# Funnel attention with a routed feed-forward: small PSUM results read by ScalarE, two transposes and the loads issued earlier, the stores of x later

## The chip, the cores and the metric

The kernel runs on one core of a Trainium2 chip. The metric is the device time of one launch in microseconds (us): the median of three runs before the change is 805.76 us (804.05 to 808.37).

## The reference

Inputs are q, k and v of shape (8, 8, 1152, 64) in fp32 (batch, heads, positions, head width), a gate vector of 512, weights w1 (512 x 1024) and w2 (1024 x 512), and a capacity of 128.

```
q_pool = q.reshape(B, H, 576, 2, 64).mean(axis=3)        # pairs of queries are averaged
attn   = softmax(q_pool @ k^T / sqrt(64)) ; out = attn @ v
x      = out with the heads side by side                 # (8, 576, 512)
per batch b:
  scores = x[b] @ w_gate
  top    = the 128 tokens with the largest scores
  x[b, top] += sigmoid(scores[top]) * (relu(x[b, top] @ w1) @ w2)
```

## The kernel before

The class `_Plain` does all the work. Its unit is a **pair** of heads of one batch: the two heads' 64 columns fill 128 partitions, so there are 8 x 4 = 32 pairs. The 576 pooled queries of a pair are cut into two **halves** of 288: the even half (s = 0) and the odd half (s = 1), 64 in all. `run` (L1098 on) goes over the halves with index h, and in iteration h it writes down, in this order:

- in an odd half, the loads of k, q and v of the pair after next (`load_pair`, ten DMAs issued by SP);
- `scores(h)`: nine chunks of 128 keys. A chunk is one matmul per head (L747, four PE instructions in the trace) into one PSUM tile of two banks; ScalarE turns it into exponentials p (L754, 128 x 576);
- `gated(h - 2)`: gate products of an earlier half summed (L861); after the odd half of a batch's last pair it also starts that batch's routing, with the DMA that copies x to the output and the tile diag (L894);
- `folded(h)`: the sums of p over the keys. POOL adds two thirds (acc, L779, three instructions), DVE folds the rest and then acc (L784, twice) and sums (L793);
- `weighted(h - 1)`: p times v (L762, 36 PE instructions), copied out of PSUM by ScalarE (av, L770); `drained(h - 1)`: a transpose (avb, L807) and the product with the gate vector on POOL (prod, L810);
- in an even half, `prepare_pair`: the sum of query pairs on POOL (qp, L726) and the transposes kT and qT on DVE (L729, L733) for the pair that comes next;
- in an even half, `normalized` of the pair just finished: one matmul that merges the sums (L822), 1e-9 added while DVE reads it out of PSUM (L832, two instructions), the reciprocal rec (L840), x on POOL (L842), and four DMAs on SP that store x to the DRAM tile xs (L850);
- `units`: one step of the routing of each batch under way.

Routing (`routed`, L876 on) is a generator that is stopped at each `yield True` until the next half. Its steps: the gate scores spread over all partitions by a matmul with ones (L905, it reads diag); the scores turned into columns by five tiny transposes (L664) that DVE reads out of PSUM (L668, L669); ranks by comparison on DVE; the pick matrix; the index matmul (L983), read out of PSUM by DVE (L991, L993), and an indirect DMA that gathers the 128 picked rows (xe, L995); their transposes (L1008); the first layer (L1019, 64 instructions) and the second (L1032, 16), DVE's sum (L1041) and an indirect DMA that scatters the rows into the output (L1049). The steps of a batch fall into the next batch's first halves, so each stands at a fixed place of every batch but the first.

Each engine runs its instructions in the order in which the program writes them; a wait on one holds what is behind it. All PSUM tiles come from one pool of four (`banks`), so a score chunk shares it with av, the merge, the columns, the index and the feed-forward. Which of the four a tile gets is settled when the program is built.

Of the kernel before, what the change touches and what calls it, by code (L numbers as in the profile page):

```python
# [10 lines left out]
P = 128  # L11
# [3 lines left out]
F32 = mybir.dt.float32  # L15
I32 = mybir.dt.int32
AF = mybir.ActivationFunctionType
ALU = mybir.AluOpType
# [516 lines left out]
class _Plain:  # L535
# [62 lines left out]
    def constants(self):  # L598
        nc, const = self.nc, self.const
# [24 lines left out]
        )  # L624
        line_f = self.ffn.tile([1, self.Sp], F32, name="sc_row")
        nc.vector.tensor_copy(line_f[:, :], line_i.rearrange("p n i -> p (n i)"))
        self.token = const.tile([P, self.NT], F32, name="token")
        self.columns(self.token, line_f, self.banks()[:, 0, :])

# [10 lines left out]
            self.merge[:, :, :], self.same[:, :].unsqueeze(1).broadcast_to([P, P // BLK, BLK])  # L640
        )

        self.meta = const.tile([P, self.B, self.NT, 3], F32, name="meta")
# [14 lines left out]

    def columns(self, to, line, ps):

        nc, NF = self.nc, self.NF
        for t in range(self.NT):
            rows = P if t < NF else self.TAIL
            nc.tensor.transpose(  # L664
                ps[0:rows, t : t + 1], line[0:1, t * P : t * P + rows], self.ident[0:1, 0:1]
            )
        nc.vector.memset(to[:, NF : NF + 1], 0.0)
        nc.vector.tensor_copy(to[:, 0:NF], ps[:, 0:NF])  # L668
        nc.vector.tensor_copy(to[0 : self.TAIL, NF : NF + 1], ps[0 : self.TAIL, NF : NF + 1])  # L669

# [146 lines left out]
    def normalized(self, pair):  # L817


        nc, hb, hp = self.nc, self.HB, pair["hp"]  # L820
# [9 lines left out]
        for j in range(2):  # L830
            rows = slice(j * self.D, (j + 1) * self.D)
            nc.vector.tensor_scalar(  # L832
                out=tot[rows, :].rearrange("p (s n) -> p s n", s=2),
                in0=ps[rows, 0 : 4 * hb].rearrange("p (s j n) -> p s j n", s=2, j=2)[:, :, j, :],
                scalar1=1e-9,
                scalar2=None,
                op0=ALU.add,
            )
# [7 lines left out]
            op=ALU.mult,  # L846
        )
        for j, ds, rows in self.quarters():
            d0 = (2 * hp + j) * self.D
            nc.sync.dma_start(  # L850
                pair["xs"][:, d0 + ds.start : d0 + ds.stop].rearrange("(i n) d -> i n d", i=BLK),
                x[rows, :, :],
            )
# [25 lines left out]
    def routed(self, b, xs, part):  # L879
# [20 lines left out]
        yield  # L900
        sc_row = ffn.tile([P, 2, self.HALF], F32, name="sc_row")
        flat = diag.rearrange("p n i -> p (n i)")
        ps = self.banks()
        for s in range(2):
# [6 lines left out]
            )  # L911
        nc.scalar.copy(sc_row[:, :, :], ps[:, :, 0 : self.HALF])
        sc_row = sc_row.rearrange("p s n -> p (s n)")
        yield True
        sc = ffn.tile([P, NT], F32, name="gate_sc")
        self.columns(sc, sc_row, self.banks()[:, 0, :])
        gate = ffn.tile([P, NT], F32, name="gate")

        nc.vector.tensor_scalar(
            out=gate[:, :], in0=sc[:, :], scalar1=-88.0, scalar2=None, op0=ALU.max  # L920
# [48 lines left out]
        for s0, w in self.slots:  # L969
# [12 lines left out]
            for t, rows in tiles:  # L982
# [7 lines left out]
            index = ffn.tile([P, 2], I32, name="index")  # L990
            nc.vector.tensor_copy(index[0:w, :], ps[0:w, 0:2])  # L991
            own_gate = ffn.tile([P, 1], F32, name="own_gate")
            nc.vector.tensor_copy(own_gate[0:w, :], ps[0:w, 2:3])  # L993
            xe = ffn.tile([P, self.Dm], F32, name="xe")
# [6 lines left out]
                oob_is_err=False,  # L1001
            )
            yield True

# [97 lines left out]
    def run(self):  # L1102
# [10 lines left out]
        for h in range(n_halves + 1):  # L1113
            if h < n_halves:
                n, s = divmod(h, 2)
                if s == 0:
                    pair = upcoming
                    if pair["hp"] == 0:
                        xs = self.dram.tile([self.Sp, self.Dm], F32, name="xs")
                        part = self.ffn.tile([P, self.NPAIR, self.QB], F32, name="part")  # L1120
                    pair.update(xs=xs, part=part)
                elif n + 2 < len(pairs):
                    loaded = self.load_pair(*pairs[n + 2])
                else:
                    loaded = None
                if h > 1:
                    next(weights, None)
                half = {"pair": pair, "s": s}
                halves.append(half)
                self.scores(half)  # L1130
                if h > 1:
                    self.gated(halves[h - 2])
                self.folded(half)
            elif h > 1:
                self.gated(halves[h - 2])
            if h > 0:
                done = halves[h - 1]
                self.weighted(done)
                self.drained(done)
            if h < n_halves and s == 0 and loaded:  # L1140
                upcoming = loaded
                self.prepare_pair(upcoming)
            if h > 0 and done["s"] == 1:
# [3 lines left out]
        for _ in weights:  # L1147
            pass


# [87 lines left out]
```

## Time and profile before

| | before |
|---|---|
| median of 3 runs | 805.76 us |
| the profiled execution, device time | 803.0 us |
| its span, first to last instruction | 801.3 us |
| TensorE (PE) busy | 760.9 us, 95% |
| VectorE (DVE) busy | 541.9 us, 68% |
| GpSimd (POOL) busy | 422.1 us, 53% |
| ScalarE (ACT) busy | 372.7 us, 47% |
| mean granted TensorE clock | 0.993 of full speed |

The profiled execution is one launch; 1.7 us of its time lie outside the span. Busy time of PE is not work at its peak, since matmuls are pipelined and a block that waits between its instructions still shows as nearly busy. So the blocks of PE are compared with each other: the same 36 instructions in one place and in another.

### The profile page before, as it was taken

The page shows a single profiled execution, that of the slowest core. Times are in us where ns is not written, and L with a number is a line of the kernel's source. Part 1 is how long each engine was busy: PE and PEld are TensorE (multiplying, and loading weights), DVE is VectorE, ACT ScalarE, POOL GpSimd, SP SyncE. Part 2 cuts the span into 40 slices and gives each one's busy share as a digit, 9 for nine tenths or more (in the row PEclk, how much of TensorE's full clock was granted, in tenths as well). Part 3 has the DMA queues.
Part 4 walks back from the last instruction along what each step waited for, and adds up shares of the span by engine and source line. Part 5 has one row for each costly group of instructions (what it writes and reads, how often), then busy time and mean ns, then how long its engine had stood idle before and what let it go on. Part 6 is the DMA issues. An engine that isn't in the chain of part 4 may idle for free.

```text
span 801.3 us, 14111 instructions
## 1 busy us (share of the span) xinstructions
PE 760.9 (95%) x5503; PEld 475.7 (59%) x5503; DVE 541.9 (68%) x888; ACT 372.7 (47%) x681; POOL 422.1 (53%) x372
## 2 busy tenths in 40 slices
PE   6999989999999999999999899998999999999896
PEld 4666546566565655657556575565755657556564
DVE  4666679964698637896288762987539876398560
ACT  5555555533555335553455444554435553355310
POOL 5666666563555636655265643665536645266320
PEclk9999999999999999999999999999999999999899
DMA  9677785567155671556725557355565555450120
GB/s 156 140 154 160 156 189 105 105 117 159 28 98 101 117 163 39 95 93 114 163 53 104 95 102 162 62 92 106 100 143 86 96 92 104 125 104 16 29 88 31
DMA packets 453643, 84.97 MB, mean 106 GB/s; under 512 B 450752, under 2 KB 450752, under 8 KB 453312
## 3 DMA queue, kind: packets, MB, share of 16 engines
q1 hardware_dynamic: 446976, 79.13, 51.8%
q0 software_dynamic: 1280, 4.20, 1.7%
q10 hardware_dynamic: 5312, 0.66, 0.5%
q8 instruction: 45, 0.74, 0.4%
q14 instruction: 30, 0.25, 0.1%
HBM read 72.42 MB, written 20.97 MB: 117 GB/s over the span
## 4 chain that ended last, share of the span: by engine, by line
PE 39%; POOL 20%; issue 18%; DVE 9%; DMA 7%; ACT 4%; SPq 3%; POOLq 0%; ACTq 0%
PE ps L747 15%; POOL acc L779 13%; PE ps L762 12%; PE ps L1019 5%; PE ps L1032 4%; POOL qp L726 4%; ACT p L754 4%; DMA xe<-xs,index 3%; DVE fold L784 2%; DMA out_dram<-xs 2%; POOL x L842 1%; POOL prod L810 1%; DVE qT L733 1%; DMA v_sb<-in_v_dram 1%; DVE part L863 1%
## 5 line engine op out<-in xcount | busy, mean ns | idle before, releaser
L754 ACT ACTIVATE p<-ps 128x576 f32<-128x576 f32 x576 | 325.8, 679 | 97.0 <-PE ps L747 48.0
L747 PE MATMUL ps<-qT,kT 64*128 64x288 f32 x2304 | 326.4, 426 | 17.9 <-ACT p L754 12.3
L762 PE MATMUL ps<-p,v_sb 128*64 128x288 f32 x2304 | 293.5, 409 | 0.0
L779 POOL TENSOR_TENSOR acc<-p 128x576 f32<-128x576 f32 x192 | 266.5, 1416 | 28.5 <-ACT p L754 28.2
L747 PEld LDWEIGHTS ps<-qT,kT 64*128 64x128 f32 x2304 | 205.1, 188 | 125.8 <-ACT p L754 71.3
L762 PEld LDWEIGHTS ps<-p,v_sb 128*64 128x64 f32 x2304 | 159.8, 137 | 125.6 <-ACT p L754 24.2
L784 DVE TRANSPOSE_TENSOR_REDUCE fold<-p 128x54 f32<-128x1728 f32 x64 | 126.1, 1970 | 78.2 <-ACT p L754 78.2
L810 POOL TENSOR_TENSOR prod<-avb,w_gate 128x288 f32<-128x288 f32 x64 | 51.0, 796 | 209.8 <-DVE avb L807 194.9
L784 DVE TRANSPOSE_TENSOR_REDUCE fold<-acc 128x54 f32<-128x1728 f32 x64 | 125.2, 1957 | 50.5 <-POOL acc L779 50.4
L770 ACT COPY av<-ps 128x288 f32<-128x288 f32 x64 | 25.5, 398 | 229.2 <-PE ps L762 229.2
L842 POOL TENSOR_TENSOR x<-avb,rec 128x576 f32<-128x576 f32 x32 | 37.0, 1157 | 44.6 <-DVE rec L840 34.4
L1019 PE MATMUL ps<-xeT,w 128*128 128x128 f32 x512 | 59.6, 276 | 0.6 <-ACT xeT L1011 0.6
L1019 PEld LDWEIGHTS ps<-xeT,w 128*128 128x128 f32 x512 | 58.0, 192 | 0.8 <-ACT xeT L1011 0.7
L1032 PE MATMUL ps<-w,hT 128*128 128x512 f32 x128 | 56.5, 593 | 0.0
L726 POOL TENSOR_TENSOR qp<-qb 128x576 f32<-128x576 f32 (+1 forms) x33 | 45.1, 1366 | 7.2 <-DMA qb<-in_q_dram 7.1
L733 DVE STREAM_TRANSPOSE qT<-qp 128x576 f32<-128x576 f32 (+1 forms) x33 | 25.1, 760 | 34.4 <-POOL qp L726 34.4
L1041 DVE SCALAR_TENSOR_TENSOR xe<-ps,own_gate,xe 128x512 f32<-128x512 f32 x8 | 6.0, 751 | 59.0 <-PE ps L1032 59.0
L1049 POOL DMA_INDIRECT out_dram<-xe,index x8 | 8.3, 1034 | 70.2 <-DMA out_dram<-xs 35.1
L729 DVE STREAM_TRANSPOSE kT<-kb 128x1152 f32<-128x1152 f32 (+1 forms) x33 | 43.0, 1302 | 3.1 <-DMA kb<-in_k_dram 3.1
L1032 PEld LDWEIGHTS ps<-w,hT 128*128 128x128 f32 x128 | 24.1, 190 | 27.0 <-issue 26.3
L861 DVE TENSOR_REDUCE red<-prod 128x9 f32<-128x288 f32 x64 | 28.0, 437 | 11.2 <-POOL prod L810 11.2
L1027 ACT ACTIVATE hT<-ps 128x512 f32<-128x512 f32 x16 | 9.6, 597 | 53.3 <-PE ps L1019 53.3
(66 smaller groups left out, 332.1 us busy)
## 6 DMA issues: line engine op xcount, KB each, us to landing
v_sb<-in_v_dram SPq DMA_DIRECT2D x64, 288.0 KB, 4.1
kb<-in_k_dram SPq DMA_DIRECT2D x124, 144.0 KB, 3.2
qb<-in_q_dram SPq DMA_DIRECT2D x124, 144.0 KB, 3.5
xs<-x SPq DMA_DIRECT2D x128, 72.0 KB, 2.2
out_dram<-xs SPq DMA_DIRECT2D x8, 1152.0 KB, 7.5
w<-in_moe_w_dram SPq DMA_DIRECT2D x8, 512.0 KB, 5.5
kb<-in_k_dram SPq DMA_DIRECT2D x8, 72.0 KB, 3.0
qb<-in_q_dram ACTq DMA_DIRECT2D x8, 72.0 KB, 3.1
```

What stands on the lines that cost most here:

```text
L726: nc.gpsimd.tensor_tensor(out=qp[:, qs, :], in0=pair["q"][:, qs, 0, :], in1=pair["q"][:, qs, 1, :], op=ALU.add)
L729: nc.vector.transpose(pair["kT"][:, i * nk * BLK : (i + 1) * nk * BLK], pair["k"][:, ks, :].rearrange("p n d -> p (n d)"),)
L733: nc.vector.transpose(pair["qT"][:, i * nq * BLK : (i + 1) * nq * BLK], qp[:, qs, :].rearrange("p n d -> p (n d)"),)
L747: nc.tensor.matmul(sc[:, j, 0:n], lhsT=pair["kT"][rows, c * P : (c + 1) * P], rhs=pair["qT"][rows, qs], start=True, stop=True,)
L754: nc.scalar.activation(p[:, c // G, c % G, :, :], sc[:, :, 0:n], AF.Exp, scale=self.scale)
L762: nc.tensor.matmul(av[j * self.D : (j + 1) * self.D, 0:n], lhsT=half["pair"]["v"][:, j, c, :], rhs=half["p"][:, c // G, c % G, j, :], star ...
L779: nc.gpsimd.tensor_tensor(out=acc[:, u, :], in0=units[:, 0, u, :], in1=units[:, 1, u, :], op=ALU.add)
L784: nc.vector.tensor_reduce(fold[:, a, :], of.rearrange("p u (m d) -> p (u m) d", d=BLK), AX.X, ALU.add, apply_transpose=True,)
L810: nc.gpsimd.tensor_tensor(out=pair["prod"][:, ns, :], in0=pair["avb"][:, ns, :], in1=self.w_gate[:, hp : hp + 1, :].broadcast_to([P, hb, B ...
L842: nc.gpsimd.tensor_tensor(out=x[:, :, :], in0=pair["avb"][:, :, :], in1=rec[:, :].unsqueeze(2).broadcast_to([P, self.QB, BLK]), op=ALU.mult,)
L1019: nc.tensor.matmul(pv[:, f, 0:w], lhsT=self.w1[:, c, (f0 + f) * P : (f0 + f + 1) * P], rhs=xeT[:, c, 0:w], start=(c == 0), stop=(c == self ...
L1032: nc.tensor.matmul(ps[0:w, 0 : self.Dm], lhsT=hT[:, f, 0:w], rhs=self.w2[:, f, :], start=(f == 0), stop=(f == self.NFC - 1),)
```

## The change

Four things are done. First, small results that DVE read out of PSUM are read by ScalarE: the merged sums (an Identity activation with a bias tile `tiny` that holds 1e-9), the columns (now five full transposes from a row of 640 whose tail POOL fills with zeros, and one copy), the index and the gate of the picked rows. The lower bound of the gate moves from DVE to POOL. Second, `prepare_pair` is called right behind the even half's `folded`, ahead of `weighted` and `drained`. Third, the stores of x become a function `stored`, called an odd half later and behind the loads; before, `normalized` issued them ahead of the loads. Fourth, routing gets one more `yield True` behind the gather, so the transposes of the picked rows and both layers come a half later, and one more call of `units` stands ahead of the last `weighted`.

```
-    def columns(self, to, line, ps):
+    def line_of_scores(self):
+        line = self.ffn.tile([P, self.NT * P], F32, name="sc_row")
+        self.nc.gpsimd.memset(line[0:1, self.Sp :], 0.0)
+        return line
+    def columns(self, to, line):
+        ps = self.banks()[:, 0, 0 : self.NT]
         for t in range(self.NT):
...
-                ps[0:rows, t : t + 1], line[0:1, t * P : t * P + rows], self.ident[0:1, 0:1]
-            )
-        nc.vector.memset(to[:, NF : NF + 1], 0.0)
-        nc.vector.tensor_copy(to[:, 0:NF], ps[:, 0:NF])
-        nc.vector.tensor_copy(to[0 : self.TAIL, NF : NF + 1], ps[0 : self.TAIL, NF : NF + 1])
+                ps[:, t : t + 1], line[0:1, t * P : (t + 1) * P], self.ident[0:1, 0:1]
+            )
+        nc.scalar.copy(to[:, :], ps)
...
     def normalized(self, pair):
-            nc.vector.tensor_scalar(
-                out=tot[rows, :].rearrange("p (s n) -> p s n", s=2),
-                in0=ps[rows, 0 : 4 * hb].rearrange("p (s j n) -> p s j n", s=2, j=2)[:, :, j, :],
-                scalar1=1e-9,
-                scalar2=None,
-                op0=ALU.add,
+            nc.scalar.activation(
+                tot[rows, :].rearrange("p (s n) -> p s n", s=2),
+                ps[rows, 0 : 4 * hb].rearrange("p (s j n) -> p s j n", s=2, j=2)[:, :, j, :],
+                AF.Identity,
+                bias=self.tiny[rows, 0:1],
             )
...
+        pair["x"] = x
+    def stored(self, pair):
         for j, ds, rows in self.quarters():
-            nc.sync.dma_start(
+            self.nc.sync.dma_start(
                 pair["xs"][:, d0 + ds.start : d0 + ds.stop].rearrange("(i n) d -> i n d", i=BLK),
-                x[rows, :, :],
+                pair["x"][rows, :, :],
             )
...
-        nc.vector.tensor_scalar(
+        nc.gpsimd.tensor_scalar(
             out=gate[:, :], in0=sc[:, :], scalar1=-88.0, scalar2=None, op0=ALU.max
         )
...
-            nc.vector.tensor_copy(index[0:w, :], ps[0:w, 0:2])
+            nc.scalar.copy(index[0:w, :], ps[0:w, 0:2])
-            nc.vector.tensor_copy(own_gate[0:w, :], ps[0:w, 2:3])
+            nc.scalar.copy(own_gate[0:w, :], ps[0:w, 2:3])
...
+            yield True
             yield True
             xeT = ffn.tile([P, self.ND, P], F32, name="xeT")
...
-                elif n + 2 < len(pairs):
-                    loaded = self.load_pair(*pairs[n + 2])
                 else:
-                    loaded = None
+                    loaded = self.load_pair(*pairs[n + 2]) if n + 2 < len(pairs) else None
+                    if n > 0:
+                        self.stored(halves[h - 2]["pair"])
...
                 self.folded(half)
+                if s == 0 and loaded:
+                    upcoming = loaded
+                    self.prepare_pair(upcoming)
             elif h > 1:
                 self.gated(halves[h - 2])
+            if h == n_halves:
+                self.units()
             if h > 0:
                 done = halves[h - 1]
                 self.weighted(done)
                 self.drained(done)
-            if h < n_halves and s == 0 and loaded:
-                upcoming = loaded
-                self.prepare_pair(upcoming)
```

On ScalarE, around the even half that turns a batch's scores into columns, before the change:

```order
L912 COPY sc_row<-ps 128x576
L754 ACTIVATE p<-ps 128x576 x9
L770 COPY av<-ps 128x288
L754 ACTIVATE p<-ps 128x576 x9
L770 COPY av<-ps 128x288
```

and of the changed program, at the same place:

```order
L920 COPY sc_row<-ps 128x576
L760 ACTIVATE p<-ps 128x576 x9
L776 COPY av<-ps 128x288
L837 ACTIVATE sums<-ps,tiny 64x18 x2
L675 COPY gate_sc<-ps 128x5
L760 ACTIVATE p<-ps 128x576 x9
L776 COPY av<-ps 128x288
```

The two reads of the merged sums and the one of the columns now stand between a copy of av and the next nine exponentials.

On VectorE, one pair of the first batch, from an even half's second fold on, before:

```order
L784 TENSOR_REDUCE fold<-acc 128x54
L793 TENSOR_REDUCE sum<-fold 128x18
L807 STREAM_TRANSPOSE avb<-av 128x288
L729 STREAM_TRANSPOSE kT<-kb 128x1152
L733 STREAM_TRANSPOSE qT<-qp 128x576
L832 TENSOR_SCALAR sums<-ps 64x18 x2
L840 RECIPROCAL rec<-sums 128x18
L861 TENSOR_REDUCE red<-prod 128x9
L863 TENSOR_TENSOR part<-red,rec 128x18
```

and of the changed program:

```order
L790 TENSOR_REDUCE fold<-acc 128x54
L799 TENSOR_REDUCE sum<-fold 128x18
L735 STREAM_TRANSPOSE kT<-kb 128x1152
L739 STREAM_TRANSPOSE qT<-qp 128x576
L813 STREAM_TRANSPOSE avb<-av 128x288
L844 RECIPROCAL rec<-sums 128x18
L869 TENSOR_REDUCE red<-prod 128x9
L871 TENSOR_TENSOR part<-red,rec 128x18
```

The transposes kT and qT moved ahead of avb, and the two reads of sums are gone from this queue.

On TensorE, the second half of a batch's routing and the start of the next one (the picked rows xe, the first layer xeT, the spread scores diag, the second layer hT, the columns sc_row), before:

```order
L1008 MATMUL ps<-ident,xe 128x128 x4
L747 MATMUL ps<-qT,kT 128x288 x18
L762 MATMUL ps<-p,v_sb 64x288 x18
L822 MATMUL ps<-sum,merge 128x36
L1019 MATMUL ps<-xeT,w_126 128x128 x32
L747 MATMUL ps<-qT,kT 128x288 x18
L762 MATMUL ps<-p,v_sb 64x288 x18
L905 MATMUL ps<-diag,ones 128x288 x2
L1032 MATMUL ps<-w_127,hT 128x512 x8
```

and of the changed program:

```order
L827 MATMUL ps<-sum,merge 128x36
L1018 MATMUL ps<-ident,xe 128x128 x4
L753 MATMUL ps<-qT,kT 128x288 x18
L768 MATMUL ps<-p,v_sb 64x288 x18
L913 MATMUL ps<-diag,ones 128x288 x2
L1029 MATMUL ps<-xeT,w_127 128x128 x32
L753 MATMUL ps<-qT,kT 128x288 x18
L768 MATMUL ps<-p,v_sb 64x288 x18
L827 MATMUL ps<-sum,merge 128x36
L672 MATMUL ps<-ident,sc_row 128x1 x5
L1042 MATMUL ps<-w_128,hT 128x512 x8
```

The first layer moved from ahead of the matmul on diag to behind it, and the second layer now stands between the columns and an odd half's scores.

## Rows read from the trace of the kernel before

**Rows 1.** The page: busy time (share of the span), instructions.

```profile
PE 760.9 (95%) x5503; PEld 475.7 (59%) x5503; DVE 541.9 (68%) x888; ACT 372.7 (47%) x681; POOL 422.1 (53%) x372
```

**Rows 2.** Timeline, PE, most of a batch: start, us, line, op, idle before.

```profile
299.73 4.64 PE L747 MATMUL ps<-qT,kT 64*128 64x288 f32 x36
...
309.51 1.24 PE L747 MATMUL ps<-qT,kT 64*128 64x288 f32 x8
311.07 1.30 PE L747 MATMUL ps<-qT,kT 64*128 64x288 f32 x8 [0.31 <-ACT p L754]
...
316.27 4.59 PE L762 MATMUL ps<-p,v_sb 128*64 128x288 f32 x36
320.79 4.72 PE L747 MATMUL ps<-qT,kT 64*128 64x288 f32 x36
...
348.85 0.41 PE L822 MATMUL ps<-sum,merge 128*128 128x36 f32 x2
349.10 1.23 PE L983 MATMUL ps<-meta,pick 128*128 128x3 f32 x9
...
357.04 4.59 PE L762 MATMUL ps<-p,v_sb 128*64 128x288 f32 x36
...
372.49 7.39 PE L1019 MATMUL ps<-xeT,w 128*128 128x128 f32 x64
379.81 5.03 PE L747 MATMUL ps<-qT,kT 64*128 64x288 f32 x36
```

**Rows 3.** Timeline, PE, the last pair's odd half.

```profile
739.66 1.23 PE L983 MATMUL ps<-meta,pick 128*128 128x3 f32 x9
...
744.68 6.04 PE L747 MATMUL ps<-qT,kT 64*128 64x288 f32 x28 [2.60 <-DVE sums L832]
750.66 1.68 PE L762 MATMUL ps<-p,v_sb 128*64 128x288 f32 x12
```

**Rows 4.** Waits: engine, line, waited for: us in total, times, longest us.

```profile
PE ps L1008 <- DMA xe<-xs,index: 7.3, 7, 1.7
PE ps L905 <- DVE diag L894: 3.6, 1, 3.6
```

**Rows 5.** Waits of SP's queue.

```profile
SPq L850 <- POOL x L842: 358.4, 32, 20.9
```

**Rows 6.** Timeline, ACT, an odd half behind the columns and a plain one.

```profile
212.72 1.19 ACT L754 ACTIVATE p<-ps 128x576 f32<-128x576 f32 x2 [1.04 <-PE ps L747]
...
233.50 5.00 ACT L754 ACTIVATE p<-ps 128x576 f32<-128x576 f32 x9 [0.68 <-PE ps L747]
```

**Rows 7.** Lines by form: busy us, mean ns of one | idle before.

```profile
L770 ACT COPY av<-ps 128x288 f32<-128x288 f32 x64 | 25.5, 398 | 229.2 <-PE ps L762 229.2
...
L832 DVE TENSOR_SCALAR sums<-ps 64x18 f32<-64x18 f32 x64 | 10.3, 162 | 0.8
...
L961 ACT ACTIVATE gate<-gate 128x5 f32<-128x5 f32 x8 | 1.7, 210 | 0.0
...
L754 ACT ACT_TABLE_LOAD x1 | 1.3, 1283 | 8.9 <-DMA qb<-in_q_dram 8.9
```

**Rows 8.** Timeline, DVE, first batch: two folds one pair apart, and diag.

```profile
65.47 1.98 DVE L784 TRANSPOSE_TENSOR_REDUCE fold<-acc 128x54 f32<-128x1728 f32 x1 [2.22 <-POOL acc L779]
...
85.07 1.98 DVE L784 TRANSPOSE_TENSOR_REDUCE fold<-acc 128x54 f32<-128x1728 f32 x1 [2.22 <-POOL acc L779]
...
97.83 0.78 DVE L733 STREAM_TRANSPOSE qT<-qp 128x576 f32<-128x576 f32 x1 [1.01 <-POOL qp L726]
...
100.89 1.59 DVE L894 TENSOR_TENSOR diag<-line,same 128x576 f32<-128x576 f32 x1
```

**Rows 9.** Timeline, POOL, beside that diag.

```profile
100.48 4.65 POOL L779 TENSOR_TENSOR acc<-p 128x576 f32<-128x576 f32 x3
```

**Rows 10.** Timeline, a later batch: diag on DVE, and PE's matmul on it.

```profile
282.05 0.76 DVE L894 TENSOR_TENSOR diag<-line,same 128x576 f32<-128x576 f32 x1
...
291.69 1.24 PE L905 MATMUL ps<-diag,ones 128*128 128x288 f32 x4
```

More of the change, by code (lines that the diff above doesn't have):

```diff
@@ L624, in constants @@
         )
-        line_f = self.ffn.tile([1, self.Sp], F32, name="sc_row")
-        nc.vector.tensor_copy(line_f[:, :], line_i.rearrange("p n i -> p (n i)"))
+        line_f = self.line_of_scores()
+        nc.vector.tensor_copy(line_f[0:1, 0 : self.Sp], line_i.rearrange("p n i -> p (n i)"))
         self.token = const.tile([P, self.NT], F32, name="token")
-        self.columns(self.token, line_f, self.banks()[:, 0, :])
+        self.columns(self.token, line_f)
         self.same = const.tile([P, BLK], F32, name="same")
@@ L641, in constants @@
         )
+        self.tiny = const.tile([P, 1], F32, name="tiny")
+        nc.gpsimd.memset(self.tiny[:, :], 1e-9)
         self.meta = const.tile([P, self.B, self.NT, 3], F32, name="meta")
@@ L657, in constants @@
         self.w2 = const.tile([P, self.NFC, self.Dm], F32, name="w2")
-    def columns(self, to, line, ps):
-        nc, NF = self.nc, self.NF
+    def line_of_scores(self):
[3 more added lines that the diff above has]
+    def columns(self, to, line):
+        nc = self.nc
+        ps = self.banks()[:, 0, 0 : self.NT]
         for t in range(self.NT):
-            rows = P if t < NF else self.TAIL
             nc.tensor.transpose(
-                ps[0:rows, t : t + 1], line[0:1, t * P : t * P + rows], self.ident[0:1, 0:1]
+                ps[:, t : t + 1], line[0:1, t * P : (t + 1) * P], self.ident[0:1, 0:1]
             )
-        nc.vector.memset(to[:, NF : NF + 1], 0.0)
-        nc.vector.tensor_copy(to[:, 0:NF], ps[:, 0:NF])
-        nc.vector.tensor_copy(to[0 : self.TAIL, NF : NF + 1], ps[0 : self.TAIL, NF : NF + 1])
+        nc.scalar.copy(to[:, :], ps)
     def load_gate(self):
@@ L847, in normalized @@
         )
+        pair["x"] = x
+    def stored(self, pair):
         for j, ds, rows in self.quarters():
-            d0 = (2 * hp + j) * self.D
-            nc.sync.dma_start(
+            d0 = (2 * pair["hp"] + j) * self.D
+            self.nc.sync.dma_start(
                 pair["xs"][:, d0 + ds.start : d0 + ds.stop].rearrange("(i n) d -> i n d", i=BLK),
-                x[rows, :, :],
+                pair["x"][rows, :, :],
             )
@@ L900, in routed @@
         yield
-        sc_row = ffn.tile([P, 2, self.HALF], F32, name="sc_row")
+        sc_row = self.line_of_scores()
         flat = diag.rearrange("p n i -> p (n i)")
@@ L911, in routed @@
             )
-        nc.scalar.copy(sc_row[:, :, :], ps[:, :, 0 : self.HALF])
-        sc_row = sc_row.rearrange("p s n -> p (s n)")
+        nc.scalar.copy(
+            sc_row[:, 0:Sp].rearrange("p (s n) -> p s n", s=2), ps[:, :, 0 : self.HALF]
+        )
         yield True
         sc = ffn.tile([P, NT], F32, name="gate_sc")
-        self.columns(sc, sc_row, self.banks()[:, 0, :])
+        self.columns(sc, sc_row)
         gate = ffn.tile([P, NT], F32, name="gate")
-        nc.vector.tensor_scalar(
+        nc.gpsimd.tensor_scalar(
             out=gate[:, :], in0=sc[:, :], scalar1=-88.0, scalar2=None, op0=ALU.max
@@ L1148, in run @@
             pass
+        self.stored(halves[-1]["pair"])
         self.gated(halves[-1])
```

## The prediction

> **What bounds the kernel now.** The page comes first: PE is busy 95% of the span, no other engine above 68% [rows 1]. So a microsecond is won only where PE's own instructions move closer together, and the second view is PE's timeline over one batch, where equal blocks are compared. An even half's scores take 4.64 us for 36 instructions [rows 2]; printed durations overlap the next instruction by 0.07 to 0.08 (4.64 here, the next block begins 4.56 later), so 4.56 is what such a block costs. The same block takes 5.03 in most odd halves. The odd half behind the columns runs from 309.51 to 316.27, 6.76: its instructions come in eights, 1.51 apart, each eight (two chunks) waiting for ScalarE's exponentials. The index matmul and the odd half behind it take from 349.10 to 357.04, 7.94. The reader is to see that PE waits only for ScalarE in these rows, yet ScalarE is not full: it needs 5.00 for nine exponentials [rows 6] and there it takes longer. I read it as the number of the four PSUM tiles that the chunks can use. Two tiles for nine chunks give pairs in lockstep; three give ScalarE's own pace of 5.0; four let PE run ahead at 4.56. The tiles that are missing are the ones that DVE reads: the merge in every odd half, with it the columns or the index in two of four. In the last odd half PE waits for that read by name, 2.60 us for sums L832 [rows 3].
>
> Then the table of waits: PE waits 7.3 us in seven places for the gathered rows, 3.6 once for diag [rows 4]. Last, the queues that nobody on PE waits for: SP stood 358.4 us, one wait a pair, in front of the stores of x, with the loads behind them [rows 5].
>
> **The change part by part**, on the profiled execution, 803.0 us (span 801.3 and 1.7 around it).
>
> *The reads go to ScalarE.* Behind the copy of av they are ready at once, the tiles come free before the first exponentials, and all four serve the chunks. Of the 31 odd halves behind a merge:
> - 17 are blocks of 5.03 like the one at 379.81: 5.03 - 4.64 = 0.39 each, 6.6 us.
> - 7 stand behind the columns, 6.76 each. The first batch's falls to 4.56, 2.20. In the other six the second layer now stands in between, and its tile is still read by DVE; I keep the three-tile pace of 4.95 for them, 1.81 each, 10.9. Together 13.1; if that tile is free too, 2.3 more.
> - 6 stand behind the index: of 7.94, 6.76 are scores as behind the columns, so 1.18 the index; 1.18 + 4.56 = 5.74, 2.20 each, 13.2. The seventh, the last odd half, takes 11.00 (739.66 to 750.66 [rows 3]) and saves 5.26. Together 18.5.
> - 7 even halves behind the columns take 4.72 instead of 4.64: 0.6.
>
> What ScalarE pays: two reads of 64 x 18 a pair and one or two small copies in the odd halves named. The nearest rows are 0.21 (128 x 5, not from PSUM) and 0.40 (128 x 288 from PSUM) [rows 7]; I take 0.21, since the sizes are near it. They stand where ScalarE is idle, 0.68 in a plain odd half and 1.04 behind the columns [rows 6]: 0.42 of 0.68, 0.63 of 1.04, so nothing. At 0.40 each, 0.80 would stick out by 0.12 in 32 places, 3.8 us. The waits that these reads add hold the exponentials behind them, but they are for matmuls that stand ahead of those scores on PE. [...]
>
> *One more half between gather and transposes.* The seven waits of 7.3 us go: a half lasts some 9 us, the longest wait was 1.7.
>
> *The transposes ahead of avb.* This works through DVE's chain, second fold, sum, avb, kT, qT, sums, rec, red, part, line, diag. In the first batch it comes round every 19.60 us (65.47 to 85.07 [rows 8]), while PE's pair takes 2 x 4.51 (316.27 to 320.79) + 4.56 + 4.95 + 0.25 for the merge (348.85 to 349.10 [rows 2]) = 18.8: DVE falls behind 0.8 a pair until PE waits 3.60 for diag. The change takes from the chain the wait of qT for qp (1.01) and the two reads (2 x 0.162 = 0.32) and adds an estimated 0.6, since red now waits for a prod that starts later; 0.7 to 0.8 less, 18.8 to 18.9. But PE's pair falls to 18.4. So DVE still falls behind by 0.45 a pair; over the four pairs the wait shrinks by 4 x 0.35 to 2.2: 1.4 saved.
>
> *What is late next: diag in every later batch.* Today none of them waits, because the first layer, 7.32 us of PE (372.49 to 379.81), stands ahead of the matmul on diag; it moves behind it. There diag is done at 282.81 and PE arrives at 291.69, 8.88 later [rows 10]; without the first layer 1.56 are left. PE also arrives earlier by what is saved in the two halves or three before, 2.20 + 0.39 + 7.3 / 7 = 3.6, DVE by two rounds of 0.75. And diag, 0.76 now, then runs beside POOL's acc, as in the first batch, where it took 1.59 [rows 8] while three acc, elsewhere 4.14, took 4.65 [rows 9]: 0.83 more. -1.56 + 3.6 - 1.5 + 0.83 = 1.4; I take 1.5 in each of six batches, 9.0 lost. Its ends are 0 and the 3.60 of the first batch. (The seventh is the program's end, where the order on PE stays.)
>
> [...]
>
> *Loads at once, stores behind them.* PE never waits for k, q or v in this stretch, so earlier loads win nothing. The stores leave some ten issues later; their reader, the gather, comes four halves on, and that is the cover. If it went, PE would wait for the rows as in [rows 4], about 1 us in seven batches. POOL's extra gate bound and fills, 8 x 0.3 and less, lie in its idle time.
>
> **Sum.** 6.6 + 13.1 + 18.5 + 0.6 + 7.3 + 1.4 - 9.0 = 38.5. 803.0 - 38.5 = 764.5. The median of the runs lies 2.8 above the profiled execution, so 767.3; I say 767.
>
> **The rivals.**
> - *DVE becomes the bound.* The round of 18.85 does not keep up with 18.4, the ranks stand in the same queue, and each of six batches waits the full 3.60: 21.6 instead of 9.0, and nothing of the first 3.60 saved. Of the gains 46.1 are left. 803.0 - 46.1 + 21.6 = 778.5, in runs 781. For it: the first batch shows it. Against it: the first layer alone gives DVE 7.3 us a batch to catch up, and DVE is rid of 10.3 us of sums and of the columns' reads.
> - *The tiles are not the reason.* Odd halves stay at 5.03 and 6.76, because ScalarE's pace sets them; then 7.3 and 1.4 are won and up to 9.0 lost: no change, 803.0, in runs 806. For it: every row of those blocks names ScalarE. Against it: even halves run at 4.56 with the same nine exponentials.
> - *ScalarE swaps its function table.* The new Identity stands between two runs of exponentials. If each change of function loaded a table at the 1.28 of [rows 7], it would be 64 loads on ScalarE, ahead of the scores' exponentials: 82 us, 764.5 + 82 = 846.5, in runs 849, slower. It decides from 38.5 / 64 = 0.60 us a change. Against it: the program before copies with ScalarE between exponentials 64 times and shows one load. [...]
>
> **How the numbers follow.** The forecast holds 0.80, DVE as the bound 0.13, tiles not the reason 0.04, tables 0.03. The forecast's own range: all waits on diag at 0, with six faster odd halves, gives 767.3 - 9.0 - 2.2 - 2.3 = 754; diag late by twice as much (9.0) and ScalarE at 0.40 (3.8) give 780. With DVE as the bound the upper end is 781. Range 754 to 781. About 0.5% is what a measurement can tell from no change; the first two cases are faster, the third is the same, the fourth slower, and I leave 0.01 more to same: faster 0.92, same 0.05, slower 0.03.
>
> **What would show it.** Right: odd halves' scores of 36 instructions at 4.64 instead of 5.03, those behind the index likewise; no wait of PE for xe; no reads of sums on DVE; ACT with one table load; PE waiting for diag in most batches, 1 to 2 us. Wrong: eights 1.51 apart that stay, more than one table load, or diag waits above 3 us. The prediction falls if ScalarE's small reads take far more than 0.4, or if the earlier loads and the ordering of POOL's work push acc, and with it the folds, behind PE so that the merge matmul itself waits.

## The result, and the profile after

The changed kernel takes **773.0 us** (median of 4 runs, 772.3 to 773.7), the kernel before 806.0 in the same round (804.1 to 808.4): ratio 0.959, 95% interval 0.956 to 0.962. The forecast was 767 with a range of 754 to 781. The profiled execution took 773.65 us with a span of 771.9, against 803.0 and 801.3; these two differ by 29.4, the medians by 33.0, since before's profiled execution lay 3.0 below its median and the changed kernel's 0.6 above.

The page answers [rows 1] so (busy us, share of the span, instructions):

```profile
PE 740.6 (96%) x5503; PEld 492.6 (64%) x5503; DVE 526.1 (68%) x773; ACT 388.0 (50%) x770; POOL 425.9 (55%) x390
```

PE is busy 20.3 us less with the same number of matmuls, ScalarE 15.3 more, DVE 15.8 less. PE's timeline over most of a batch answers [rows 2 and 10] (start, us, line, op, idle before):

```profile
237.19 4.63 PE L753 MATMUL ps<-qT,kT 64*128 64x288 f32 x36
...
246.27 0.41 PE L827 MATMUL ps<-sum,merge 128*128 128x36 f32 x2
246.51 1.23 PE L992 MATMUL ps<-meta,pick 128*128 128x3 f32 x9
...
252.26 4.59 PE L768 MATMUL ps<-p,v_sb 128*64 128x288 f32 x36
...
277.68 1.21 PE L913 MATMUL ps<-diag,ones 128*128 128x288 f32 x4 [1.86 <-DVE diag L902]
278.72 7.31 PE L1029 MATMUL ps<-xeT,w 128*128 128x128 f32 x64
...
295.38 0.47 PE L672 MATMUL ps<-ident,sc_row 1*128 1x1 f32 x5
295.78 7.13 PE L1042 MATMUL ps<-w,hT 128*128 128x512 f32 x16
302.84 5.03 PE L753 MATMUL ps<-qT,kT 64*128 64x288 f32 x36
```

From the index matmul to the next weighted products is 5.75 us where it was 7.94. The odd half that follows both the columns and the second layer is at 5.03, still ScalarE's pace (5.00 for nine exponentials). The new stop is in front of diag's matmul. The waits, which answer [rows 3 and 4]:

```profile
PE ps L913 <- DVE diag L902: 11.4, 6, 2.3
PE ps L753 <- DVE qT L739: 7.4, 2, 4.2
...
PE ps L1018 <- DMA xe<-xs,index: 1.0, 2, 0.7
```

No row of PE names the sums any more. On ScalarE the reads appear, with one table load, against [rows 7]; and SP's queue, against [rows 5], now stands in front of the loads, since the keys' buffer is not yet transposed:

```profile
L837 ACT ACTIVATE sums<-ps,tiny 64x18 f32<-64x18 f32 x64 | 17.4, 272 | 1.0
...
L675 ACT ACT_TABLE_LOAD x1 | 1.3, 1283 | 5.3 <-DMA qb<-in_q_dram 5.3
```

```profile
SPq L705 <- DVE kT L735: 223.0, 31, 12.9
SPq L858 <- POOL x L846: 33.3, 2, 16.9
```

What the prediction had no term for stands at the program's start, PE again. Before, the second scores began at 23.39 and the first merge at 32.47, without a gap. In the changed kernel:

```profile
8.76 11.18 PE L753 MATMUL ps<-qT,kT 64*128 64x288 f32 x72 [4.21 <-DVE qT L739]
19.87 4.59 PE L768 MATMUL ps<-p,v_sb 128*64 128x288 f32 x36
27.62 7.53 PE L753 MATMUL ps<-qT,kT 64*128 64x288 f32 x36 [3.17 <-DVE qT L739]
35.08 4.59 PE L768 MATMUL ps<-p,v_sb 128*64 128x288 f32 x36
39.60 0.41 PE L827 MATMUL ps<-sum,merge 128*128 128x36 f32 x2
```

The first merge is 7.1 us late. And SP's DMA queue (packets, MB, share of 16 engines' time), with the landing time of a pair's quarter of the keys, moved the same bytes in much more engine time; before, the share was 51.8% and the landing 3.2 us:

```profile
q1 hardware_dynamic: 446976, 79.13, 69.7%
...
kb<-in_k_dram SPq DMA_DIRECT2D x124, 144.0 KB, 4.6
```

Block by block on PE (start of a block to start of the next, from the two timelines):

| what | places | before | forecast | after |
|---|---|---|---|---|
| plain odd halves | 17 | 4.95 | 4.56 | 4.57 |
| odd half, first batch's columns | 1 | 6.77 | 4.56 | 4.57 |
| odd half, later columns | 6 | 6.76 | 4.95 | 4.95 (one 5.23) |
| index + odd half | 6 | 7.94 | 5.74 | 5.75 |
| the same, last | 1 | 11.00 | 5.74 | 5.74 |
| waits for gathered rows, in all | 7 | 7.3 | 0 | 1.0 |
| wait for diag, first batch | 1 | 3.6 | 2.2 | 0 |
| waits for diag, later, in all | 6 | 0 | 9.0 | 11.4 |
| first merge begins at | 1 | 32.47 | no term | 39.60 |

The differences, 6.5 + 2.2 + 10.6 + 13.1 + 5.3 + 0.6 (even halves behind columns) + 6.3 + 3.6 - 11.4 - 7.1, make 29.7, where the spans differ by 29.4.

### The profile page after: what moved, and what is told of

Its sections match the earlier page's. It is cut to its first block, busy times and chain, and to the rows that moved or that the text cites. A ratio compares the mean times of both kernels' runs of the same rounds, so it can differ in the third digit from the quotient of the medians.

```text
span 771.9 us, 14195 instructions
## 1 busy us (share of the span) xinstructions
PE 740.6 (96%) x5503; PEld 492.6 (64%) x5503; DVE 526.1 (68%) x773; ACT 388.0 (50%) x770; POOL 425.9 (55%) x390
## 3 DMA queue, kind: packets, MB, share of 16 engines
q1 hardware_dynamic: 446976, 79.13, 69.7%
## 5 line engine op out<-in xcount | busy, mean ns | idle before, releaser
L760 ACT ACTIVATE p<-ps 128x576 f32<-128x576 f32 x576 | 320.3, 684 | 66.9 <-issue 48.0
L753 PE MATMUL ps<-qT,kT 64*128 64x288 f32 x2304 | 305.8, 416 | 7.5 <-DVE qT L739 7.4
L753 PEld LDWEIGHTS ps<-qT,kT 64*128 64x128 f32 x2304 | 221.8, 189 | 80.7 <-issue 22.0
L732 POOL TENSOR_TENSOR qp<-qb 128x576 f32<-128x576 f32 (+1 forms) x33 | 45.0, 1365 | 11.4 <-DMA qb<-in_q_dram 11.4
L982 DVE TENSOR_SCALAR pick<-slot_f,rank 128x128 f32<-128x128 f32 (+1 forms) x40 | 37.9, 1012 | 0.3
L813 DVE STREAM_TRANSPOSE avb<-av 128x288 f32<-128x288 f32 x64 | 29.0, 453 | 1.0 <-ACT av L776 1.0
L1059 POOL DMA_INDIRECT out_dram<-xe,index x8 | 8.5, 1067 | 38.0 <-DVE xe L1051 34.8
```

The source lines that it names most:

```text
L732: nc.gpsimd.tensor_tensor(out=qp[:, qs, :], in0=pair["q"][:, qs, 0, :], in1=pair["q"][:, qs, 1, :], op=ALU.add)
L753: nc.tensor.matmul(sc[:, j, 0:n], lhsT=pair["kT"][rows, c * P : (c + 1) * P], rhs=pair["qT"][rows, qs], start=True, stop=True,)
L760: nc.scalar.activation(p[:, c // G, c % G, :, :], sc[:, :, 0:n], AF.Exp, scale=self.scale)
L982: nc.vector.tensor_scalar(out=pick[0:rows, t, 0:w], in0=self.slot_f[0:rows, s0 : s0 + w], scalar1=rank[0:rows, t : t + 1], scalar2=None, o ...
```

## The experiments

Twelve kernels ran. Each is compared with runs of the kernel before on the same chip (medians 804.2, 805.6 and 805.4 on three occasions, 806.0 beside the changed kernel). A difference between two edited kernels can cross two occasions, and then 1 to 2 us of it mean little. Traces show one execution of each.

**The kernel before once more**, unedited, to see whether start and long packets belong to the chip.

> The unchanged kernel once more, for its trace. The changed kernel's first merge stood at 39.60 us, this one's at 32.47 in the first trace, and its DMA packets took some 30% longer in all of the program. Theory A, ScalarE's queue at the start (the read of the token columns and the table load ahead of the last loads of q): here the first scores begin at 7.5 and the first merge stands at 32.5 again. Theory B, slower DMA in that execution whatever the kernel: here too the packets are long, the first scores begin near 8.8 and the first merge comes near 35 to 39.

805.6 us in its one run, first merge at 32.38, the queue's share:

```profile
q1 hardware_dynamic: 446976, 79.13, 51.5%
```

So the chip does not bring them by itself; both came with the changed kernel.

**Token copy on VectorE**, since ScalarE's first table load and first read now stand ahead of the last two of its loads of queries.

```
-        self.columns(self.token, line_f)
+        self.columns(self.token, line_f, nc.vector.tensor_copy)
```

> The changed kernel, but the token columns at the start are read out of PSUM by VectorE, as before the change, so that ScalarE's queue does not stop there. Theory A: the 7.1 us at the start come back, 773 becomes 766, first merge near 33. Theory B: no change, 772 to 774, first merge near 39.

773.7 us, ratio 0.962 (0.961 to 0.964). In the profiled execution, the fastest of five (770.8), the first merge came at 34.83, but the share stayed at 68.9%, and the first batch now waited 1.5 for diag: 4.8 us earlier at the start, nothing won in the median. The copy is not what lengthens the packets. That its move brought the earlier start is not shown, since the start differs by 5 us between other kernels that do not differ in the copy (34.19 and 39.27, below).

**The older batch's layers first**, so that the first layer covers diag, as before the change.

```
-        for unit in self.routing[::-1]:
+        for unit in list(self.routing):
```

> The changed kernel, but each half's routing steps run for the older batch first, so the first layer (7.2 us of PE) stands ahead of the matmul on diag again. Theory (diag waits exist because the first layer moved behind that matmul): the six waits of 11.4 us go, 773 becomes 761 to 762. Rival (VectorE is the bound and only shows up at diag): PE waits as long somewhere else, 771 to 775.

760.6 us, ratio 0.945 (0.944 to 0.947), 12.4 below the changed kernel, with the start as late as there (39.40). PE's timeline of the same stretch has the first layer ahead of diag's matmul and no wait; diag is gone from the table of waits:

```profile
268.58 4.59 PE L768 MATMUL ps<-p,v_sb 128*64 128x288 f32 x36
273.10 7.41 PE L1029 MATMUL ps<-xeT,w 128*128 128x128 f32 x64
280.34 1.14 PE L913 MATMUL ps<-diag,ones 128*128 128x288 f32 x4
```

The diag term was real, and it was a price of the order on PE, not of the reads.

**Without the added half between gather and transposes**, and without the added call of `units` at the end.

```
-            yield True
             yield True
...
-            if h == n_halves:
-                self.units()
```

> The changed kernel without the added half between gather and transposes (and without the added call of units at the end). The diag waits (11.4) go, since the first layer stands ahead again, and the odd half behind the columns falls from 4.95 to 4.56 (2.3). Theory (the half is needed more after the change than before, since PE reaches the transposes 2.2 us earlier): the wait for the gathered rows becomes 1.1 + 2.2 = 3.3 in seven places, 23 us, so 773 + 23 - 14 = 782. Rival (the wait stays what it was, 7.3 in all): 773 + 7 - 14 = 766.

799.7 us, ratio 0.994 (0.993 to 0.996): nearly all of the gain gone, far more than expected, although the first layer stands ahead of diag's matmul again and only 1.5 of the waits for diag is left. Waits, then PE at one place, then the granted clock beside it (busy of PE, PEld, DVE, ACT, POOL; clock; DMA share; GB/s):

```profile
PE ps L1017 <- DMA xe<-xs,index: 27.3, 7, 4.8
```

```profile
167.53 1.09 PE L1017 MATMUL ps<-ident,xe 128*128 128x128 f32 x4 [4.79 <-DMA xe<-xs,index]
168.55 6.88 PE L753 MATMUL ps<-qT,kT 64*128 64x288 f32 x36
```

```profile
163.00:168.00 5.00, 0.47 (x3) 0.50 (x4) 1.27 (x2) 0.19 (x1) 4.56 (x4) 0.83 1.27 169
168.00:173.00 5.00, 5.00 (x21) 3.46 (x22) 2.78 (x4) 2.73 (x5) 0.79 (x1) 0.50 1.44 180
```

The wait is paid twice: 4.79 of idle PE, and then a granted clock of 0.50 from 168 to 173 us, in which the next scores take 6.88 instead of 4.63. Six places go this way, with waits of 4.1 to 4.8 and scores of 5.5 to 7.1 behind them. The shorter the blocks, the earlier PE arrives: 1 us a place became 4.

**The reads alone** (sums, columns and index to ScalarE, the gate's maximum to GpSimd; all order as before; `tiny` of 16 floats, see below). Against the kernel before, without the lines for sums and columns that the change's own diff shows:

```
-            nc.vector.tensor_copy(index[0:w, :], ps[0:w, 0:2])
+            nc.scalar.copy(index[0:w, :], ps[0:w, 0:2])
-            nc.vector.tensor_copy(own_gate[0:w, :], ps[0:w, 2:3])
+            nc.scalar.copy(own_gate[0:w, :], ps[0:w, 2:3])
```

> The kernel before with only the reads of the small PSUM results moved to ScalarE (sums, columns, index) and the gate's maximum on GpSimd; `tiny` of 16 floats; the transposes, the loads and stores and the steps of the routing stay as before. Theory (the tiles of PSUM came back late because VectorE read them): the odd blocks behind a merge take 4.57 us and not 4.96, the blocks with the index 5.75 and not 7.94, without anything else of the change. What this gives is then partly taken back by the gathered rows, which are wanted one block after their index as in the run without the added half of a batch (4 us of waiting in 7 places and a clock of 0.50 for some 5 us behind it): 780 to 798 us. Rival (the moved transposes made the blocks short): odd blocks stay at 4.8 to 4.96, index blocks at over 7, 800 to 806 us.

796.8 us, ratio 0.990 (0.987 to 0.992). On PE a plain odd half and an index block:

```profile
229.91 4.64 PE L754 MATMUL ps<-qT,kT 64*128 64x288 f32 x36
234.48 4.59 PE L769 MATMUL ps<-p,v_sb 128*64 128x288 f32 x36
...
248.32 1.23 PE L990 MATMUL ps<-meta,pick 128*128 128x3 f32 x9
...
254.07 4.59 PE L769 MATMUL ps<-p,v_sb 128*64 128x288 f32 x36
```

The plain odd halves take 4.57, those behind the columns 4.57, index and odd half 5.75, the last 5.74. Only the first routing's index block is long, 8.51: PE waits 0.97 for pick in it. So the reads alone shorten the blocks, by some 38 us in all. Most of it is taken back by the gather, 21.8 us of waits in eight places (7.3 before) and scores of 5.8 to 7.0 behind six of them. The added half is what turns the gain into time.

**Where the tiles lie.** `tiny` is a constant of one float, yet by the allocation's rounding, as I reckon it, all that lies behind it (keys, queries, values, x, weights, gathered rows) moves by 32 bytes of each partition; no trace prints the addresses. First the kernel before with that constant alone, read by nobody:

```
+        self.tiny = const.tile([P, 1], F32, name="tiny")
+        nc.gpsimd.memset(self.tiny[:, :], 1e-9)
```

> The kernel before with only the constant `tiny` added (one float, 32 bytes of each partition), written once and read by nobody. Theory C: the SP queue's share rises from 51.7% to 68 to 71%, the quarters of the keys land in 4.4 to 4.7 us, the first merge moves from 32.4 to 37 to 40 us, and the time from 804 to 808 to 813 us. Rival (the order of the stores and loads): nothing changes, 51 to 53%, 32.4 us, 803 to 807.

808.5 us, ratio 1.003 (1.001 to 1.005), first merge at 35.20, and

```profile
q1 hardware_dynamic: 446976, 79.13, 64.6%
...
v_sb<-in_v_dram SPq DMA_DIRECT2D x64, 288.0 KB, 5.2
kb<-in_k_dram SPq DMA_DIRECT2D x124, 144.0 KB, 4.4
```

The place alone lengthens the transfers: a quarter of the keys lands in 4.4 us and not 3.2, the values in 5.2 and not 4.1, and the queue's share grows by a quarter. The changed kernel's 69.7% is still more, and that rest is not explained. The stores, which read x out of a tile that moved too, do not change (2.3 us against 2.2). I took multiples of 64 bytes for the rule, and that was wrong. The changed kernel with 16 floats:

```
-        self.tiny = const.tile([P, 1], F32, name="tiny")
+        self.tiny = const.tile([P, 16], F32, name="tiny")
```

> The changed kernel with one edit: the new constant `tiny` is allocated as 16 floats in each partition instead of one, so that what is allocated behind it (keys, queries, values, x, the weights, the gathered rows) lies at multiples of 64 bytes again, as before the change, and not 32 bytes beside them. Theory C (the place of the tiles in SBUF lengthens the transfers): the SP queue's share of 16 engines falls from 69.7% back to 50 to 54%, a quarter of the keys lands in 3.2 us and not 4.6, the first merge of sums is at 33 to 36 us and not 39.6, and the time is 764 to 770 us. Rival (the stores' and loads' new order makes the transfers meet each other): the share stays at 68 to 71%, the first merge at 39 to 40 us, the time at 773 (+-1).

771.0 us, ratio 0.957 (0.956 to 0.959); first merge at 34.19, but

```profile
q1 hardware_dynamic: 446976, 79.13, 67.3%
```

A shift of 64 is nearly as bad as one of 32 (64.6% with the order of before, in the run with the reads alone). Then the kernel before with `tiny` of 128 bytes, unread:

```
+        self.tiny = const.tile([P, 32], F32, name="tiny")
+        nc.gpsimd.memset(self.tiny[:, 0:1], 1e-9)
```

> The kernel before with `tiny` of 32 floats added and read by nobody: all behind it lies 128 bytes further, at the same place modulo 128 and off by half modulo 256. If 128 bytes are what counts: the SP queue's share stays at 51 to 53%, the first merge at 32.4 us, 803 to 807 us. If 256 bytes count, or the exact place: 63 to 66%, the first merge at 34 to 35.5 us, 806 to 810 us.

805.7 us, ratio 1.000 (0.998 to 1.001), first merge 32.84:

```profile
q1 hardware_dynamic: 446976, 79.13, 52.2%
...
v_sb<-in_v_dram SPq DMA_DIRECT2D x64, 288.0 KB, 4.4
kb<-in_k_dram SPq DMA_DIRECT2D x124, 144.0 KB, 3.3
```

So of these three shifts the one by 128 bytes left the keys and queries, whose rows are 32 floats, 128 bytes, nearly as they were: the keys landed in 3.3 us against 4.4 at 32 and, in the run with the reads alone, 4.2 at 64, the queries in 3.6 against 4.6 and 4.4 (before: 3.2 and 3.5). The values, with rows of 256 bytes, landed in 4.4 at 128, nearer to the 4.1 of before than to the 5.2 at 32 and the 5.0 at 64. The stores of x, where the moved tile is read, grew no longer at any of the three (2.3, 2.3 and 2.2 against 2.2). Why the place matters to a transfer is not shown.

**Order and place together.**

```
-        for unit in self.routing[::-1]:
+        for unit in list(self.routing):
...
+        self.tiny = const.tile([P, 16], F32, name="tiny")
```

> The changed kernel with `tiny` of 16 floats and, as in the run with the older batch's routing unit first, the units started in their written order, so that the older batch's layers go ahead of the younger batch's diagonal. If both reasons hold and add up: no wait for the diagonal, 50 to 54% of the SP queue, the first merge at 33 to 36 us, and 760.6 less 4 to 7 = 753 to 757 us. If the place of the tiles doesn't matter: 760 to 761. If the shorter transfers had only moved waiting from one place to another, as the run with the token copy on VectorE did: 758 to 762 with the first merge early.

758.7 us, ratio 0.942 (0.940 to 0.944), first merge at 34.06, one wait for diag of 1.5 in the first batch. The third expectation fits: of 5.3 us by which the profiled starts differ, 1.9 arrive in the medians (two occasions).

**Order, place and token copy**: the units' order as there, and

```
-        self.tiny = const.tile([P, 1], F32, name="tiny")
+        self.tiny = const.tile([P, 64], F32, name="tiny")
...
+        self.columns(self.token, line_f, nc.vector.tensor_copy)
```

> The changed kernel with three edits: the routing's units in their written order, the column of token numbers copied by VectorE, and `tiny` of 64 floats, so that everything behind it lies 256 bytes further than before the change and at the same place modulo 256 (with 64 bytes of shift the SP queue's share stayed at 67%). Theory C in a new form (the packets are longer where a tile lies off its place modulo 128 or 256 bytes): the share falls to 50 to 56%, the quarters of the keys land in 3.2 to 3.5 us, the first merge is at 32 to 33 us, and the time is 752 to 757 us. Rival (the exact place decides, or the order of loads and stores): 66 to 70%, first merge at 33.5 to 35, 756 to 760.

**755.3 us**, ratio 0.938 (0.936 to 0.940), the fastest measured, 17.7 below the changed kernel. Share 55.5%, keys 3.2 us, values 4.1; the 3 to 4 points that are left above before's share are not explained. Which of the place and the copy brings the early start is not separated here. The start is that of before:

```profile
7.52 11.21 PE L753 MATMUL ps<-qT,kT 64*128 64x288 f32 x72 [2.96 <-DVE qT L739]
18.66 4.59 PE L768 MATMUL ps<-p,v_sb 128*64 128x288 f32 x36
23.17 4.64 PE L753 MATMUL ps<-qT,kT 64*128 64x288 f32 x36
```

**Transposes back behind the weighted products**, with 64 bytes, so against 771.0.

```
-                if s == 0 and loaded:
-                    upcoming = loaded
-                    self.prepare_pair(upcoming)
...
                 self.drained(done)
+            if h < n_halves and s == 0 and loaded:
+                upcoming = loaded
+                self.prepare_pair(upcoming)
```

> The changed kernel with `tiny` of 16 floats (771.0 us) and the preparation of the next pair put back behind the weighted products, where it stood before. Theory (its place behind an even half's folds only keeps VectorE's chain ahead of the diagonal short; the blocks owe nothing to it): odd blocks stay at 4.57 us and index blocks at 5.75, the six blocks behind the second layer return from 4.95 to 4.57 us, and the waits for the diagonal grow from 12.9 us to 18 to 30: 774 to 788 us. Rival (the place of the transposes is what made the blocks short): odd blocks at 4.8 to 4.96 again in 11 and more places, 779 to 785 by these alone. Second rival (no effect): 770 to 772.

784.4 us, ratio 0.973 (0.971 to 0.975). Odd halves 4.57 and index blocks 5.74: they owe nothing to this move. The waits for diag grow from 12.9 to 17.3 in 7 places, and the first layer behind six of them takes 8.6 to 8.9 instead of 7.2; in the second of the six, 281.0 to 289.9, the granted clock was 0.84 from 283 to 288 us. That is 4.4 and some 9.6 us, and the time is 13.4 longer. The five instructions on pick (see the next run) take 4.27 here. The blocks behind the second layer stayed at 4.95, against my expectation.

**Stores back into the step that makes x**, ahead of the next loads; against 771.0.

```
         pair["x"] = x
+        self.stored(pair)
...
-                    if n > 0:
-                        self.stored(halves[h - 2]["pair"])
...
-        self.stored(halves[-1]["pair"])
```

> The changed kernel with `tiny` of 16 floats (771.0 us) and the stores of x put back into the step that makes x, ahead of the next loads on SP's queue. Theory (the loads and the stores are hidden in either order, as the prediction costed them at nothing): 769.5 to 772.5 us, the SP queue's share 63 to 68%. Rival (loads that no longer stand behind a wait for x keep the keys' transposes early): 774 to 780 us, with waits for keys or queries in the middle of the program and larger waits for the diagonal.

**765.9 us**, ratio 0.949 (0.947 to 0.952): 5 us faster, where theory and rival had 0 and a loss, though this execution had the late start again (39.27). The waits for diag, with 64 bytes and then with the stores back as well:

```profile
PE ps L913 <- DVE diag L902: 12.9, 7, 2.4
```

```profile
PE ps L914 <- DVE diag L903: 6.9, 6, 2.6
```

The first has 1.5 in the first batch, which the late start hides in the second; in the six later batches 11.4 fell to 6.9. A wait of 1.0 for pick in the first routing went too. The cause is on DVE and GpSimd. In the changed kernel the five instructions on pick (DVE), and the GpSimd work beside them:

```profile
241.48 5.43 DVE L982 TENSOR_SCALAR pick<-slot_f,rank 128x128 f32<-128x128 f32 x5
```

```profile
241.16 4.12 POOL L785 TENSOR_TENSOR acc<-p 128x576 f32<-128x576 f32 x3
245.25 1.39 POOL L732 TENSOR_TENSOR qp<-qb 128x576 f32<-128x576 f32 x1
```

With the stores first, the queries land later, so qp leaves pick alone:

```profile
241.47 4.27 DVE L983 TENSOR_SCALAR pick<-slot_f,rank 128x128 f32<-128x128 f32 x5
```

```profile
241.15 4.12 POOL L785 TENSOR_TENSOR acc<-p 128x576 f32<-128x576 f32 x3
247.29 1.40 POOL L732 TENSOR_TENSOR qp<-qb 128x576 f32<-128x576 f32 x1 [2.02 <-DMA qb<-in_q_dram]
```

Pick is 1.16 shorter, all behind it on DVE comes earlier by that, and the transposes lose only 0.50 to a late qp later in the batch:

```profile
271.89 0.78 DVE L739 STREAM_TRANSPOSE qT<-qp 128x576 f32<-128x576 f32 x1 [0.50 <-POOL qp L732]
```

So pick's time changed with what GpSimd did beside it; at the end of the changed program, with GpSimd idle, the same five take

```profile
744.03 1.06 DVE L982 TENSOR_SCALAR pick<-slot_f,rank 128x128 f32<-128x128 f32 x5
```

One qp lasts 1.39, and 1.16 is most of it; why qp lengthens pick is not shown.

## Why the prediction was right or wrong

**Right: the reads.** *The reads go to ScalarE*: 17 plain halves, the first columns block, six kept at 4.95, six index blocks and the last came out within 0.01 us each but for one, and the run with the reads alone shows them as the cause. That the link is the number of free PSUM tiles fits the eights 1.51 apart and the wait for sums in [rows 3], but no run changed the number of tiles by itself. For the 4.95 behind the second layer the reason given (its tile, still read by DVE) is not shown, and the kernel before speaks against it. There the second layer stands ahead of an even half, DVE reads its tile just as promptly, and that half takes 4.56 (299.73 to 304.29). DVE's read before and after:

```profile
299.83 0.75 DVE L1041 SCALAR_TENSOR_TENSOR xe<-ps,own_gate,xe 128x512 f32<-128x512 f32 x1 [7.12 <-PE ps L1032]
```

```profile
302.95 0.75 DVE L1051 SCALAR_TENSOR_TENSOR xe<-ps,own_gate,xe 128x512 f32<-128x512 f32 x1 [2.46 <-PE ps L1042]
```

Moving the transposes back did not change the 4.95 either; with the reads alone, where the second layer does not stand between, it is 4.57. So the number came true and its reason stays open.

**Right: the table and the reads' price.** One table load. The read of sums took 272 ns, not the 210 assumed: two are 0.56 (as the timeline prints a pair) and stood in the idle time of [rows 6].

**Right in kind, too small by far in price: the gather's half.** Its waits went, 6.3 of the 7.3. But its worth beside the shorter blocks is 26.7 us (799.7 against 773.0), the waits for diag that come with it already taken off, since without it PE stands 4.1 to 4.8 us at six places and takes 5.5 to 7.1 for the scores behind them.

**Mis-sized: diag.** *What is late next* gave 9.0 for six batches, measured 11.4, and 2.2 for the first, measured none, because PE itself is late there (1.4 to 1.5 in the traces with an early start and this order of the transposes). The 1.59 beside acc [rows 8] was the right length for diag (1.59 or 1.60 in the first seven of eight). What the sum left out is that two parts of the change together bring qp beside pick. *The transposes ahead of avb* puts qp right behind acc on GpSimd, and loads that no longer stand behind the stores have its rows there in time. *Loads at once, stores behind them* said that earlier loads win nothing and took their cost as nothing too. With either part undone pick takes 4.27 and not 5.43, and DVE, on whose chain diag hangs, is earlier by that. Putting the stores back took 4.6 us of waits away in the six later batches, and 5.0 of time.

**Missed: the start.** No step had a term for it, and 7.1 us were lost. `tiny` cost nothing as an instruction (805.7 with 128 bytes of it, beside 805.4), but it moved the tiles: the kernel before, moved by the same 32 bytes, begins its first merge 2.7 later (35.20). The rest is seen but not explained. In the changed kernel qT of the second pair came late, PE stood 3.17 us, and the scores behind ran 7.5 us; the granted clock was 0.83 from 20 to 30 us and 0.82 from 30 to 40. Two more traces have this start (39.40 and 39.27). In the others with 32 or 64 bytes the first merge is at 34.0 to 34.8, and without the added half at 36.86: there PE stood 3.45, yet the clock stayed at 1.00 and the scores took 4.56. Part of the loss is given back at diag in the first batch.

**The rivals.** *DVE becomes the bound* came half true: from diag to diag a later batch lasts 93.6 us (182.30 to 275.93), and with the older batch first, where nothing waits for diag, 91.6; but a wait is 1.9, not 3.6. That the layers give DVE time to catch up, as the prediction held against this rival, fits, and no run tests it by itself. *The tiles are not the reason* and *ScalarE swaps its function table* fell.

The total, 29.4 on the profiled executions against 38.5 forecast, is short by 7.1 for the start and 2.4 for diag, by 1.0 at the gather and 0.8 in other rows, less 2.2 won at the first diag. That the median, 773.0, came only 6 above the 767 is in part luck: the forecast added 2.8, by which before's median lay above its profiled execution, and the changed kernel's median lay 0.6 below its own. And the room of the range up to 781 was meant for DVE and ScalarE; the start used it.

**Left open.** What the stores' place is worth with the older batch first was not run; no wait for diag is left there to shorten. Why the same start is sometimes 2 us and sometimes 7 us late is seen only as PE's gap and clock, not explained. So is what holds the halves behind the second layer at 4.95.

## What to carry to other kernels

Count the buffers that a pipelined engine can use, and ask who frees each of them: a short read by a busy engine can cost more than its length (here DVE's reads of the sums and the columns, 0.14 to 0.16 us each, and 2.2 us in the odd half behind them, 6.76 against 4.57 with the reads on ScalarE). A gain in blocks moves every arrival, so each deadline behind it (here gather and diag) has to be moved in the same change (without the added half the waits for gathered rows were 27.3 us, before the change 7.3). And look at the addresses: a tile of one float, placed ahead of others, can shift all that transfers write to (the keys landed in 4.4 us and not 3.2).

## What the runs showed of the hardware

- The keys' transfers into SBUF, rows of 128 bytes, landed a third later when their tile was moved by 32 or 64 bytes, and not when it was moved by 128 (4.4 and 4.2 against 3.2 to 3.3 us; share of the queue 64.6% against 51.5 to 52.2%). The kernel before lost 0.3% by 32 bytes. The stores of x, rows of 128 bytes, out of a tile moved by 32 bytes took no longer (2.3 against 2.2).
- In the run without the added half, after 4.8 us without matmuls, the granted clock was 0.50 in the next 5 us, and a block of 4.57 took 6.81 (printed as 6.88); over the six such places of that run the blocks behind the waits lost half as much again (12.3 us beside 26.9 of waits). After 3.45 us without matmuls at the start of the same run the clock stayed at 1.00.
- Five short DVE instructions (`tensor_scalar`, four of 128 x 128 and one of 64 x 128) took 1.06 us with GpSimd idle, 4.27 beside three GpSimd additions, and 5.43 with a fourth GpSimd instruction beside them.
